# Tables built on Vector, head pairs transposed whole and Pool's mask product dropped in the first block of an attention + GLU kernel

## The chip, the cores and the metric

One core of one Trainium2 chip. The metric is the device time of one execution in microseconds; the number before is the median of four runs. One further execution was recorded by the hardware profiler; where the text gives a moment ("at 18.05"), it is counted in microseconds from the start of that execution's span.

## The reference

Two layers, one after the other. The first is a linear attention with decay, 4 batches, 8 heads, 768 positions, head dimension 64, one decay `lam` per head:

```python
for b in range(nb):                                   # blocks of positions
    intra = einsum('bhic,bhjc->bhij', qb, kb) * Dmask     # lam ** (i - j), lower triangle
    intra = einsum('bhij,bhjd->bhid', intra, vb)
    inter = einsum('bhid,bhde->bhie', qb * lam_pow, kv_state)   # lam ** (i + 1)
    out[:, :, sl] = intra + inter
    kv_state = lam_block * kv_state + einsum('bhsd,bhse->bhde', kb * rev_pow, vb)
```

The second takes the attention's output as 3072 tokens of width 512:

```python
gate = 1 / (1 + exp(-(x @ w_gate)))       # 512 x 1536
return (gate * (x @ w_val)) @ w_out       # 1536 x 512, float32
```

## The kernel before

Positions go in six units of 128 (`n` = 0 to 5, the text also says Block 0, unit 1 and so on), all four batches in each. The order of the instructions on every engine is the order in which the program writes them down; nothing reorders them.

**Attention of one unit.** q and k are transposed, so that the head dimension lies on the partitions: heads in two halves of 64 partitions (`u`), and per half four heads. `QS` is q transposed and scaled by `lamq` (lam to the power position + 1), `KS` k transposed. `piece_s` multiplies them into `sp0` and `sp1` (one per `u`, 128 x 512 each), `piece_m` multiplies by `mask` into `MT`, `piece_a` or `piece_a0` (Block 0, which has no state yet) multiplies with v and copies the result to `XT`. `make_kd` scales k for the state, `c` adds it to the state `Sb`, `fade` decays the state by `dec`.

**GLU of one unit.** For each of twelve column slices `ft` of 128: four matmuls with `WG` into `gp` (L399, L413 or L434), a sigmoid on Scalar, four with `WV` into `vp` (L405, L413, L440), the product `ht` on Vector. Then `piece_po` multiplies `ht` with `WO` and stores.

**Block 0** is written out by hand (L473 to L513), to get TensorE to the weights early. q's first two batches come as float32 by the Scalar and SP queues (`q0f`, `q1f`) and are cast by Vector; all else comes through Pool's queue, which converts to bfloat16 on the way, in this order: k batches 0-1, four Pool operations that build `jn`, `ident`, `ip1` and `tri` (L131 to L136), k 2-3, q 2, q 3, v 0, v 1, v 2, WG columns 0-127, v 3, WV columns 0-127. Further down in Pool's queue come the mask product of L282 (`piece_m2`: for batch 1, half `u` = 1, Scalar copies the scores to SBUF and Pool multiplies), then WG and WV columns 128-255 and the following slices, `make_kd(0)`, and unit 1's q, k and v.

`idle(n)` issues n matmuls of zeros, whose result nobody reads. `transpose` turns one head (128 x 64) at a time, two into the two halves of the result:

```python
def head(g, u):
    return 4 * (g % 2) + 2 * u + g // 2
```

With this order of heads `lamq`, `mask`, `MT` and the transposed tensors have one layout in all units. Units 1 (second half) and later are transposed by DMA on SP's queue (`transpose_half`, `transpose_by_dma`, L207: `QR` and `KR`), because their q and k are loaded with even and odd heads apart.

The tables: `jn` holds -1 - p and 127 - p by partition p; `ip1` is 1 to 128 along the free dimension; Scalar makes `lnp`, `lamq` (four exponentials), `lnl`, `pk`, `kds`, `dec` of them, and Vector multiplies `tri` by `pk` into `mask`.

Of the kernel before, what the change touches and what calls it, by code (L numbers as in the profile page):

```python
# [7 lines left out]

FP32 = mybir.dt.float32
BF16 = mybir.dt.bfloat16  # L10
AF = mybir.ActivationFunctionType
ALU = mybir.AluOpType
# [4 lines left out]
def kernel(  # L17
# [11 lines left out]
    nc = tc.nc  # L29

    B, H, S, D = q.shape
    C = 128
    NSTEP = S // C
    HP = H // 2
# [7 lines left out]
    const = ctx.enter_context(tc.tile_pool(name="const", bufs=1))  # L42
# [3 lines left out]
    mtp = ctx.enter_context(tc.tile_pool(name="mtp", bufs=4))  # L46
# [12 lines left out]
    lam_bc = const.tile([128, H], FP32, tag="lam_bc")  # L59
    nc.sync.dma_start(out=lam_bc, in_=lam.partition_broadcast(128))  # L60

    WG = const.tile([128, NMT, DFF], BF16, tag="WG")
    WV = const.tile([128, NMT, DFF], BF16, tag="WV")
    WO = const.tile([128, NFT, DM], BF16, tag="WO")
    wg_r = moe_w_gate.rearrange("(mt p) f -> p mt f", p=128)
    wv_r = moe_w_val.rearrange("(mt p) f -> p mt f", p=128)
    wo_r = moe_w_out.rearrange("(ft p) m -> p ft m", p=128)

    Q, K, V = {}, {}, {}
# [31 lines left out]
    def load_w(t, src, i, w):  # L101
        fs = slice(i * w, (i + 1) * w)
        nc.gpsimd.dma_start(out=t[:, :, fs], in_=src[:, :, fs])  # L103

    def load_gv(i, w):
        load_w(WG, wg_r, i, w)
        load_w(WV, wv_r, i, w)
# [5 lines left out]
    q01 = [const.tile([128, H, D], FP32, tag=f"q{b}f", name=f"q{b}f") for b in range(2)]  # L113
# [4 lines left out]
    ident = const.tile([128, 128], BF16, tag="ident")  # L118
    zero = const.tile([128, TCH], BF16, tag="zero")
    jn = const.tile([128, 2], FP32, tag="jn")  # L120
    ip1 = const.tile([128, C], FP32, tag="ip1")
    tri = const.tile([128, C], FP32, tag="tri")
    nc.vector.memset(zero, 0.0)
    nc.vector.memset(ident, 0.0)
    nc.vector.memset(tri, 0.0)
    Sb = stp.tile([128, B, HP, D], BF16, tag="Sb", name="Sb")
    nc.vector.memset(Sb, 0.0)

    load(0, "k", 0, 2)
    for i, base in enumerate((-1, C - 1)):  # L130
        nc.gpsimd.iota(jn[:, i:i + 1], pattern=[[0, 1]], base=base, channel_multiplier=-1,  # L131
                       allow_small_or_imprecise_dtypes=True)
    make_identity(nc, ident, nomemset=True)
    nc.gpsimd.iota(ip1, pattern=[[1, C]], base=1, channel_multiplier=0,
                   allow_small_or_imprecise_dtypes=True)
    nc.gpsimd.affine_select(out=tri, in_=tri, compare_op=ALU.is_gt, fill=1.0, base=0,  # L136
                            pattern=[[-1, C]], channel_multiplier=1)
    load(0, "k", 2, 4)
    load(0, "q", 2, 3)
    load(0, "q", 3, 4)  # L140
# [3 lines left out]
    GW = DFF // 6  # L144
    load_w(WG, wg_r, 0, GW // 2)
    load(0, "v", 3, 4)
    load_w(WV, wv_r, 0, GW // 2)

    lnp = const.tile([128, HP], FP32, tag="lnp")
    for u in range(2):  # L150
        us = slice(u * 64, (u + 1) * 64)
        nc.scalar.activation(lnp[us, :].rearrange("p (e x) -> p e x", e=2),
                             lam_bc[us, :].rearrange("p (x u e) -> p u e x", u=2, e=2)[:, u], AF.Ln)
    lamq = const.tile([128, HP, C], BF16, tag="lamq")
    for hp in range(HP):
        nc.scalar.activation(lamq[:, hp, :], ip1, AF.Exp, scale=lnp[:, hp:hp + 1])
    lnl = const.tile([128, H], FP32, tag="lnl")
    nc.scalar.activation(lnl, lam_bc, AF.Ln)
    pk = const.tile([128, H], FP32, tag="pk")
    nc.scalar.activation(pk, lnl, AF.Exp, scale=jn[:, 0:1])  # L160
    kds = const.tile([128, H], FP32, tag="kds")
    nc.scalar.activation(kds, lnl, AF.Exp, scale=jn[:, 1:2])
    dec = const.tile([128, HP], FP32, tag="dec")
    nc.scalar.activation(dec, lnp, AF.Exp, scale=float(C))
    nc.scalar.preload_act_table_set("sigmoid_and_others")
    mask = const.tile([128, 2, HP, C], FP32, tag="mask")

    def make_mask(u):
        nc.vector.tensor_tensor(
            out=mask[:, u].rearrange("p (e x) c -> p e x c", e=2),  # L170
            in0=tri.unsqueeze(1).unsqueeze(1).to_broadcast([128, 2, 2, C]),
            in1=pk.rearrange("p (x u e) -> p u e x", u=2, e=2)[:, u].unsqueeze(3).to_broadcast([128, 2, 2, C]),
            op=ALU.mult)

    def half(e):
        return slice(e * 64, (e + 1) * 64)
# [4 lines left out]
    def transpose(out, x, b, g):  # L181
        for u in range(2):
            nc.tensor.transpose(out[half(u)], x[:, b, head(g, u), :], ident)
# [3 lines left out]
    def idle(n):  # L187
        for i in range(n):
            nc.tensor.matmul(wm, lhsT=zero[:, :128], rhs=zero, start=True, stop=True,
                             skip_group_check=True)  # L190

    QS, KS, MT, XT, KD = {}, {}, {}, {}, {}
# [17 lines left out]
            KS[n, bp] = kt[:, :, 2 * bp:2 * bp + 2]  # L210

    lamq_e = lamq.rearrange("p (e x) c -> p e (x c)", e=2)

    def scale(n, bp, src):
        QS[n, bp] = trsb.tile([128, 2, 2, 2, C], BF16, tag="QS", name="QS")
# [4 lines left out]
    def piece_tq0(bs, then=None):  # L220
        tq = ps_at.tile([128, 2, 2, 2 * C], BF16, name="tq", tag="ps")
        for b in bs:
            if (0, b // 2) not in QS:
                QS[0, b // 2] = trsb.tile([128, 2, 2, 2, C], BF16, tag="QS", name="QS")
            for g in range(HP):
                transpose(tq[:, b % 2, g // 2, g % 2 * C:g % 2 * C + C], Q[0], b, g)
        if then:
            then()
        for b in bs:
            nc.vector.tensor_tensor(out=QS[0, b // 2][:, :, b % 2].rearrange("p e x c -> p e (x c)"),  # L230
                                    in0=tq[:, b % 2], in1=lamq_e, op=ALU.mult)

    def piece_tk0(bp):
        tk = ps_at.tile([128, 2, 2, 2 * C], BF16, name="tk", tag="ps")
        for i in range(2):
            for g in range(HP):
                transpose(tk[:, i, g // 2, g % 2 * C:g % 2 * C + C], K[0], 2 * bp + i, g)
        KS[0, bp] = trsb.tile([128, 2, 2, 2, C], BF16, tag="KS", name="KS")
        for i in range(2):
            cp = nc.vector.tensor_copy if bp == 0 and i == 0 else nc.scalar.copy  # L240
            cp(KS[0, bp][:, :, i].rearrange("p e x c -> p e (x c)"), tk[:, i])
# [18 lines left out]
    SP = {}  # L260
# [11 lines left out]
                                     start=(hp == 0), stop=(hp == HP - 1), skip_group_check=True)  # L272
            SP[n, b] = sp

    def piece_m2(n, b, part):
        if part:
            nc.vector.tensor_tensor(out=MT[n, b][:, 0], in0=SP[n, b][0], in1=mask[:, 0], op=ALU.mult)
            return
        MT[n, b] = mtp.tile([128, 2, HP, C], BF16, tag="MT", name="MT")
        sc = const.tile([128, HP, C], FP32, tag="sc", bufs=2)  # L280
        nc.scalar.copy(sc, SP[n, b][1])
        nc.gpsimd.tensor_tensor(out=MT[n, b][:, 1], in0=sc, in1=mask[:, 1], op=ALU.mult)  # L282

    def piece_m(n, b):
        MT[n, b] = mtp.tile([128, 2, HP, C], BF16, tag="MT", name="MT")
        for u in range(2):
            nc.vector.tensor_tensor(out=MT[n, b][:, u], in0=SP[n, b][u], in1=mask[:, u], op=ALU.mult)  # L287

    def intra(n, b, out, m, start, stop):
        for e in range(2):  # L290
            nc.tensor.matmul(out[half(e)], lhsT=V[n][:, b, 2 * m + e, :],  # L291
                             rhs=MT[n, b][:, m % 2, 2 * e + m // 2, :],
                             start=start, stop=stop, skip_group_check=True)

    def piece_a(n, pairs):
# [23 lines left out]
    def piece_a0(b, split=False):  # L319
        if 0 not in XT:  # L320
            XT[0] = xtp.tile([128, NMT, B, C], BF16, tag="XT", name="XT")
        w = 2 if split else NMT
        for m0 in range(0, NMT, w):
            op = ps_at.tile([128, w, C], FP32, name="op", tag="ps")
            for m in range(w):
                intra(0, b, op[:, m, :], m0 + m, m == 0, m == w - 1)
            if split and m0:
                nc.vector.tensor_copy(XT[0][:, m0:m0 + w, b, :], op)
            else:
                nc.scalar.copy(XT[0][:, m0:m0 + w, b, :], op)  # L330
# [139 lines left out]
            nc.sync.dma_start(out=out[lo:lo + rows, :], in_=ob[i * rows:(i + 1) * rows, :])  # L470


    idle(10)  # L473
    nc.vector.tensor_copy(Q[0][:, 0], q01[0])
    piece_tq0([0])
    nc.vector.tensor_copy(Q[0][:, 1], q01[1])
    idle(1)
    piece_tq0([1], lambda: make_mask(0))
    make_mask(1)
    idle(1)  # L480
    piece_tk0(0)
    idle(1)
    piece_s(0, [0])
    piece_m(0, 0)
    piece_s(0, [1])
    piece_m2(0, 1, 0)
    piece_m2(0, 1, 1)
    load_w(WG, wg_r, 1, GW // 2)
    load_w(WV, wv_r, 1, GW // 2)
    load_gv(1, GW)  # L490
    load_gv(2, GW)
    piece_tk0(1)
    piece_tq0([2])
    idle(1)
    piece_tq0([3])
# [3 lines left out]
    piece_m(0, 3)  # L499
    piece_a0(0)  # L500
    piece_a0(1)
    idle(1)
    piece_a0(2, True)
    idle(1)
    g0 = psum()
    mm_part(g0, WG, 0, 0, 0, 3 * C)
    piece_a0(3, True)
# [28 lines left out]
    def gv(n, *fts):  # L536
        for ft in fts:
            piece_gv(n, ft)
# [3 lines left out]
            piece_gvh(n, ft, i)  # L542

    gv(0, 1)
    gs = {}
    for ft in (2, 3):
        gs[ft] = psum()
# [115 lines left out]
```

## Time and profile before

| | |
|---|---|
| median of 4 runs | 228.12 us (227.67 to 228.4) |
| the profiled execution | 227.94 us, span 226.2 us |
| granted TensorE clock | 1.0 |
| TensorE busy | 217.5 us, 96% of the span |
| Vector, Scalar, Pool busy | 98.5, 79.3, 82.9 us |
| matmuls L399, L405, L462 (128x512) | 57.9, 57.6, 61.3 us, 379 ns each as recorded |
| mask products L287 on Vector | 46 of 682 ns |
| mask product L282 on Pool | 1 of 1352 ns, at 11.39 |
| TensorE's first matmul of L399 | at 18.05 us |
| last step of the chain of waits | L456 on Vector, at 223.28 us |

A line of a timeline reads: start in us, length in us, engine, line of the program, operation, result and operands, shape, count; in brackets the idle time of the engine just before it and what ended that. "PE" is TensorE's matmuls, "PEld" its weight loads, "DVE" Vector, "ACT" Scalar, "POOL" GpSimd, "SPq" the SP queue. Matmuls overlap in their recorded lengths, so their pace is read from starts, not from lengths. A group of matmuls may show fewer than it has, where records are missing.

### The profile page before, as it was taken

The page shows a single profiled execution, that of the slowest core. Times are in us where ns is not written, and L with a number is a line of the kernel's source. Part 1 is how long each engine was busy: PE and PEld are TensorE (multiplying, and loading weights), DVE is VectorE, ACT ScalarE, POOL GpSimd, SP SyncE. Part 2 cuts the span into 40 slices and gives each one's busy share as a digit, 9 for nine tenths or more (in the row PEclk, how much of TensorE's full clock was granted, in tenths as well). Part 3 has the DMA queues.
Part 4 walks back from the last instruction along what each step waited for, and adds up shares of the span by engine and source line. Part 5 has one row for each costly group of instructions (what it writes and reads, how often), then busy time and mean ns, then how long its engine had stood idle before and what let it go on. Part 6 is the DMA issues. An engine that isn't in the chain of part 4 may idle for free.

```text
span 226.2 us, 4318 instructions
## 1 busy us (share of the span) xinstructions
PE 217.5 (96%) x1772; PEld 114.8 (51%) x1796; DVE 98.5 (44%) x167; ACT 79.3 (35%) x149; POOL 82.9 (37%) x82
## 2 busy tenths in 40 slices
PE   7779999999999999999999999999999999999994
PEld 2444445788864445444446444446444445444443
DVE  2772647476422532445642335842334850343300
ACT  5544243435432225333115433225333224433221
POOL 7999987993394006940005950000000000000000
DMA  6999999999999994999221899921930012100022
GB/s 110 151 163 193 168 189 157 141 191 176 156 114 173 221 209 113 192 158 149 10 93 49 184 147 148 35 82 61 165 68 0 3 46 96 46 0 0 0 96 94
DMA packets 105861, 25.72 MB, mean 114 GB/s; under 512 B 95985, under 2 KB 102897, under 8 KB 105841
## 3 DMA queue, kind: packets, MB, share of 16 engines
q0 software_dynamic: 81232, 13.90, 95.8%
q1 hardware_dynamic: 23568, 11.28, 22.8%
q10 hardware_dynamic: 1040, 0.26, 0.5%
q8 instruction: 14, 0.23, 0.5%
q14 instruction: 7, 0.05, 0.1%
HBM read 28.32 MB, written 6.29 MB: 153 GB/s over the span
## 4 chain that ended last, share of the span: by engine, by line
PE 66%; DMA 17%; POOL 11%; SPq 2%; DVE 2%; issue 1%; DVEq 0%
PE po L462 22%; PE gp L399 19%; PE vp L405 18%; DMA qb<-in_q_dram 6%; DMA KR<-kb 5%; DMA kb<-in_k_dram 4%; SPq L207 2%; POOL WV L103 2%; PE sp L270 2%; POOL WG L103 2%; DMA q0f<-in_q_dram 2%; PE op L291 2%; POOL kd L337 2%; PE po L451 1%; PE op L303 1%; POOL WO L111 1%
## 5 line engine op out<-in xcount | busy, mean ns | idle before, releaser
L408 DVE TENSOR_TENSOR ht<-sg,vp 128x512 bf16<-128x512 bf16 x57 | 39.2, 687 | 68.7 <-PE vp L405 64.6
L462 PE MATMUL po<-WO,ht 128*128 128x512 bf16 x266 | 61.3, 379 | 0.5
L399 PE MATMUL gp<-XT,WG 128*128 128x512 bf16 x221 | 57.9, 379 | 1.0 <-DMA WG<-in_moe_w_gate_dram 0.4
L405 PE MATMUL vp<-XT,WV 128*128 128x512 bf16 x223 | 57.6, 379 | 0.1
L402 ACT ACTIVATE sg<-gp 128x512 bf16<-128x512 f32 x57 | 34.0, 597 | 62.9 <-PE gp L399 61.7
L462 PEld LDWEIGHTS <-ht 128*128 128x128 bf16 x276 | 26.3, 98 | 31.0
L405 PEld LDWEIGHTS <-WV 128*128 128x128 bf16 x228 | 22.3, 98 | 26.9
L399 PEld LDWEIGHTS <-WG 128*128 128x128 bf16 x228 | 21.7, 98 | 26.2 <-DMA WG<-in_moe_w_gate_dram 0.6
L287 DVE TENSOR_TENSOR MT<-sp,mask 128x512 bf16<-128x512 f32 x46 | 29.0, 682 | 8.7 <-PE sp L270 8.7
L465 ACT COPY ob<-po 128x512 f32<-128x512 f32 x23 | 13.5, 586 | 52.5 <-PE po L462 48.6
L364 POOL TENSOR_TENSOR sd<-Sb,dec 128x512 f32<-128x512 bf16 x8 | 8.1, 1037 | 40.8 <-DVE Sb L390 40.8
L434 PE MATMUL gp<-XT,WG 128*128 128x256 bf16 x96 | 14.4, 273 | 0.0
L440 PE MATMUL vp<-XT,WV 128*128 128x256 bf16 x96 | 14.4, 273 | 0.0
L444 DVE TENSOR_TENSOR ht<-sg,vp 128x256 bf16<-128x256 bf16 x24 | 10.0, 420 | 8.6 <-PE vp L440 8.6
L437 ACT ACTIVATE sg<-gp 128x256 bf16<-128x256 f32 x24 | 9.2, 384 | 12.6 <-PE gp L434 11.5
L97 POOL DMA_DIRECT2D vb<-in_v_dram x10 | 12.8, 1290 | 1.7 <-issue 1.1
L355 POOL TENSOR_TENSOR kd<-kb,kds 128x1024 bf16<-128x1024 bf16 x6 | 11.3, 1907 | 4.7 <-PE vp L440 4.7
L390 DVE TENSOR_TENSOR Sb<-cp,sd 128x512 bf16<-128x512 f32 x8 | 5.2, 686 | 15.5 <-PE cp L383 15.5
L317 ACT CAST XT<-op 128x512 bf16<-128x512 f32 x20 | 10.4, 597 | 3.0 <-PE op L291 3.0
L434 PEld LDWEIGHTS <-WG 128*128 128x128 bf16 x96 | 9.2, 98 | 1.7 <-issue 0.2
L440 PEld LDWEIGHTS <-WV 128*128 128x128 bf16 x96 | 9.4, 98 | 1.1
L78 POOL DMA_DIRECT2D qb<-in_q_dram x8 | 9.4, 1182 | 0.0
(77 smaller groups left out, 142.0 us busy)
## 6 DMA issues: line engine op xcount, KB each, us to landing
out_dram<-ob SPq DMA_DIRECT2D x21, 256.0 KB, 2.0
kb<-in_k_dram POOLq DMA_DIRECT2D x11, 256.0 KB, 9.7
qb<-in_q_dram POOLq DMA_DIRECT2D x9, 256.0 KB, 8.6
vb<-in_v_dram POOLq DMA_DIRECT2D x4, 512.0 KB, 14.8
WO<-in_moe_w_out_dram POOLq DMA_DIRECT2D x3, 512.0 KB, 9.1
WG<-in_moe_w_gate_dram POOLq DMA_DIRECT2D x5, 256.0 KB, 7.0
WV<-in_moe_w_val_dram POOLq DMA_DIRECT2D x5, 256.0 KB, 7.6
qb<-in_q_dram POOLq DMA_DIRECT2D x4, 128.0 KB, 7.8
```

Source lines behind the costliest of these rows:

```text
L97: nc.gpsimd.dma_start(out=lst[n][:, b0:b1], in_=src[b0:b1, :, sl, :].rearrange("b h s d -> s (b h) d"))
L287: nc.vector.tensor_tensor(out=MT[n, b][:, u], in0=SP[n, b][u], in1=mask[:, u], op=ALU.mult)
L317: nc.scalar.copy(XT[n][:, u::2, 2 * bp:2 * bp + 2, :], OP[bp, u])
L355: nc.gpsimd.tensor_tensor(out=KD[n][:, e], in0=K[n][:, e], in1=kds[:, e::2].unsqueeze(1).unsqueeze(3).to_broadcast([128, B, HP, D]), op=AL ...
L399: nc.tensor.matmul(gp, lhsT=WG[:, mt, fs], rhs=x[:, mt, :], start=(mt == 0), stop=(mt == NMT - 1))
L402: nc.scalar.activation(sg, gp, AF.Sigmoid)
L405: nc.tensor.matmul(vp, lhsT=WV[:, mt, fs], rhs=x[:, mt, :], start=(mt == 0), stop=(mt == NMT - 1))
L408: nc.vector.tensor_mul(HT[n, ft], sg, vp)
L434: nc.tensor.matmul(gp[:, cs], lhsT=WG[:, mt, fs], rhs=x[:, mt, cs], start=(mt == 0), stop=(mt == NMT - 1))
L440: nc.tensor.matmul(vp[:, cs], lhsT=WV[:, mt, fs], rhs=x[:, mt, cs], start=(mt == 0), stop=(mt == NMT - 1))
L462: nc.tensor.matmul(po, lhsT=HT[n, ft][:, tt * 128:(tt + 1) * 128], rhs=WO[:, ft, :], start=(ft == 0), stop=(ft == NFT - 1))
L465: nc.scalar.copy(ob, po)
```

## The change

1. `jn`, `ident`, `ip1` and `tri` are built on Vector instead of Pool: `ip1` by seven doubling additions from a column of ones, the partition index `p1` from a 32x32 block transpose of it and four additions, the rest by comparison with `p1`. The memsets of `ident`, `tri` and `Sb` go.
2. WG and WV columns 128-255 and the two slices after them are issued directly behind the loads, and Pool's mask product (`piece_m2`) is gone: batch 1 uses `piece_m` as the others do.
3. Block 0 keeps the natural order of heads: neighbouring heads 2g and 2g + 1 are transposed in one 128x128 transpose (`transpose_pair`). It has its own `lamq0`; the later units' `lamq` is made on Vector by doubling products (`make_lamq`), after `gv(0, 1)`. `mask` lies in natural order too, and later units read it through a strided view (`masked`).
4. Scalar casts q's second batch, its sigmoid table is loaded after the first K copies, `make_mask(0)` moves ahead of the first QS product, `piece_a0(2)` is no longer split in two, and the idle matmuls are set anew.

```diff
-    nc.vector.memset(ident, 0.0)
-    nc.vector.memset(tri, 0.0)
     Sb = stp.tile([128, B, HP, D], BF16, tag="Sb", name="Sb")
-    nc.vector.memset(Sb, 0.0)
+    nc.vector.memset(ip1[:, 0:1], 1.0)
+    w = 1
+    while w < C:
+        nc.vector.tensor_scalar_add(ip1[:, w:2 * w], ip1[:, 0:w], float(w))
+        w *= 2
+    loc = const.tile([128, 32], FP32, tag="loc")
+    nc.vector.transpose(loc, ip1[:, 0:32])
+    p1 = const.tile([128, 1], FP32, tag="p1")
+    for lo in range(0, 128, 32):
+        nc.vector.tensor_scalar_add(p1[lo:lo + 32], loc[lo:lo + 32, 0:1], float(lo))
+    nc.vector.tensor_scalar(out=ident, in0=ip1, scalar1=p1, scalar2=None, op0=ALU.is_equal)
+    for i, base in enumerate((0.0, float(C))):
+        nc.vector.tensor_scalar(out=jn[:, i:i + 1], in0=p1, scalar1=-1.0, scalar2=base,
+                                op0=ALU.mult, op1=ALU.add)
+    nc.vector.tensor_scalar(out=tri, in0=ip1, scalar1=p1, scalar2=None, op0=ALU.is_ge)
 
     load(0, "k", 0, 2)
-    for i, base in enumerate((-1, C - 1)):
-        nc.gpsimd.iota(jn[:, i:i + 1], pattern=[[0, 1]], base=base, channel_multiplier=-1,
...
-    make_identity(nc, ident, nomemset=True)
-    nc.gpsimd.iota(ip1, pattern=[[1, C]], base=1, channel_multiplier=0,
...
-    nc.gpsimd.affine_select(out=tri, in_=tri, compare_op=ALU.is_gt, fill=1.0, base=0,
...
     load_w(WV, wv_r, 0, GW // 2)
+    load_w(WG, wg_r, 1, GW // 2)
+    load_w(WV, wv_r, 1, GW // 2)
+
     lnl = const.tile([128, H], FP32, tag="lnl")
     nc.scalar.activation(lnl, lam_bc, AF.Ln)
     pk = const.tile([128, H], FP32, tag="pk")
     nc.scalar.activation(pk, lnl, AF.Exp, scale=jn[:, 0:1])
...
+        nc.scalar.activation(lnp[us, :], lam_bc[us, u::2], AF.Ln)
+    lamq0 = const.tile([128, HP, C], BF16, tag="lamq0")
+    for hp in range(HP):
+        nc.scalar.activation(lamq0[:, hp, :], ip1, AF.Exp, scale=lnp[:, hp:hp + 1])
+    nc.scalar.copy(Q[0][:, 1], q01[1])
...
-    nc.scalar.activation(dec, lnp, AF.Exp, scale=float(C))
-    nc.scalar.preload_act_table_set("sigmoid_and_others")
-    mask = const.tile([128, 2, HP, C], FP32, tag="mask")
+    for u in range(2):
+        us = slice(u * 64, (u + 1) * 64)
+        nc.scalar.activation(dec[us, :].rearrange("p (e x) -> p e x", e=2),
...
+    mask = const.tile([128, H, C], FP32, tag="mask")
+
+    def make_lamq():
+        lp = const.tile([128, HP, C], FP32, tag="lp")
+        for u in range(2):
+            us = slice(u * 64, (u + 1) * 64)
+            nc.vector.tensor_copy(lp[us].rearrange("p (e x) c -> p e x c", e=2)[:, :, :, 0],
...
+        w = 1
+        while w < C:
+            nc.vector.tensor_tensor(out=lp[:, :, w:2 * w], in0=lp[:, :, 0:w],
+                                    in1=lp[:, :, w - 1:w].to_broadcast([128, HP, w]), op=ALU.mult)
+            w *= 2
+        nc.vector.tensor_copy(lamq, lp)
...
+    def masked(out, x, n, u):
+        if n == 0:
+            nc.vector.tensor_tensor(out=out, in0=x, in1=mask[:, u::2, :], op=ALU.mult)
+            return
+        nc.vector.tensor_tensor(
+            out=out.rearrange("p (e x) c -> p e x c", e=2), in0=x.rearrange("p (e x) c -> p e x c", e=2),
+            in1=mask.rearrange("p (x u e) c -> p u e x c", u=2, e=2)[:, u], op=ALU.mult)
...
+    def transpose_pair(out, x, b, g):
+        nc.tensor.transpose(out, x[:, b, 2 * g:2 * g + 2, :].rearrange("p h d -> p (h d)"), ident)
...
-    def piece_m2(n, b, part):
...
+    load_gv(1, GW)
+    load_gv(2, GW)
+
     idle(10)
     nc.vector.tensor_copy(Q[0][:, 0], q01[0])
-    piece_tq0([0])
-    nc.vector.tensor_copy(Q[0][:, 1], q01[1])
-    idle(1)
-    piece_tq0([1], lambda: make_mask(0))
+    piece_tq0([0], lambda: make_mask(0))
     make_mask(1)
     idle(1)
+    piece_tq0([1])
     piece_tk0(0)
     idle(1)
     piece_s(0, [0])
     piece_m(0, 0)
     piece_s(0, [1])
-    piece_m2(0, 1, 0)
-    piece_m2(0, 1, 1)
-    load_w(WG, wg_r, 1, GW // 2)
-    load_w(WV, wv_r, 1, GW // 2)
-    load_gv(1, GW)
-    load_gv(2, GW)
+    piece_m(0, 1)
     piece_tk0(1)
+    nc.scalar.preload_act_table_set("sigmoid_and_others")
+    idle(1)
     piece_tq0([2])
...
-    idle(1)
-    piece_a0(2, True)
-    idle(1)
+    idle(2)
+    piece_a0(2)
+    idle(2)
     g0 = psum()
...
     gv(0, 1)
+    make_lamq()
     gs = {}
```

## The prediction

> **What bounds the kernel now.** First the page: TensorE is busy in 96% of the span, and its busy strip is full from the third slice on.
>
> ```profile
> PE 217.5 (96%) x1772; PEld 114.8 (51%) x1796; DVE 98.5 (44%) x167; ACT 79.3 (35%) x149; POOL 82.9 (37%) x82
> ...
> PE   7779999999999999999999999999999999999994
> ...
> DMA  6999999999999994999221899921930012100022
> ...
> q0 software_dynamic: 81232, 13.90, 95.8%
> ...
> q8 instruction: 14, 0.23, 0.5%
> ```
>
> So a change in Block 0 (the first 18 us) can only move the start of one long TensorE run. Where does that run wait? The timeline of TensorE, then of its weight loads:
>
> ```profile
> 17.28 0.39 PE L413 MATMUL gp<-XT,WV 128*128 128x128 bf16 x4
> 18.05 1.04 PE L399 MATMUL gp<-XT,WG 128*128 128x512 bf16 x4 [0.38 <-DMA WG<-in_moe_w_gate_dram]
> 18.92 1.03 PE L405 MATMUL vp<-XT,WV 128*128 128x512 bf16 x4
> ...
> 19.96 0.55 PEld L413 LDWEIGHTS <-WG 128*128 128x128 bf16 x4 [0.51 <-DMA WG<-in_moe_w_gate_dram]
> ...
> 74.91 0.45 PEld L270 LDWEIGHTS <-KR 64*128 64x128 bf16 x16 [0.63 <-DMA KR<-kb]
> ```
>
> All three are transfers. By issue times the gaps are: 17.50 (last of v0, 17.445 plus a pitch of 0.056) to 18.05, 0.54 us; 19.78 to 19.97, 0.19; and 74.62 (48 matmuls of 0.216 from 64.25) to 74.91, 0.29. Together 1.02 us; after that the chain of waits shows TensorE alone. The chain also says that the third gap hangs on transfers, not on TensorE:
>
> ```profile
> 30.45 9.54 DMA kb<-in_k_dram
> 39.99 0.07 issue
> 40.06 2.06 POOL kd L349 x2
> ...
> 63.66 11.21 DMA KR<-kb
> 74.87 0.05 issue
> 74.91 0.62 PE sp L270 x16
> ```
>
> Then the DMA side. The packet records show the software queue carrying about 600 packets of 128 B, or 190 of 512 B, per 0.5 us without a hole from 4.5 to 41 us. It is saturated: issuing earlier does not make it deliver earlier. The sixteen completions of each transfer add one thing. Up to the first WV slice the last of the sixteen comes 0.2 us after the median (16.35 against 16.21). From the next slice, WG's columns 128 to 255, it is 1.36 late (18.00 against 16.64), and stays over 1 late until 41 us. What happened between:
>
> ```profile
> q0 software_dynamic: 207, 0.05, 173.3%
> q8 instruction: 1, 0.02, 25.9%
> ```
>
> That is the DMA view at 15.3 to 15.6 us: one 16 KB instruction packet at 15.45, lasting 1.24 us, on an engine that carries the weights. The two early gaps are that packet.
>
> **The change, part by part.** The sum is made against the profiled execution, 227.94 us (span 226.2 and 1.74 around it), 0.18 under the median of 228.12.
>
> *Tables.* Pool loses two iotas for jn, the ident select, the ip1 iota and the tri select (2.63 to 3.49, 0.86 us); Vector loses the memsets of ident, tri and Sb (0.11 + 0.17 + 0.48) and gains 17 small operations: a memset, seven doublings, the transpose, four offsets, ident, two jn, tri. Nearest rows: the 128x64 memset at 0.11 and the 128x128 one at 0.165. At 0.11 to 0.2 each they end between 3.0 and 4.5; Vector then waits for q0f until 5.00. Nothing; at 0.25 each it would be 0.4 us late. No gain either.
>
> A rule speaks against this part. Pool's first K issue lasts 1.28 us beside Vector's memsets and the second, alone, 1.19: 0.09 for the overlap. The Trainium skill ("SBUF — State Buffer", "SBUF: two separate sides") says that a Vector operation in a two-port mode locks GpSimd out of their shared port, so that it can't write descriptors; the next section there ("A bandwidth-pool intuition that's wrong (but worth ruling out)") has a DMA of about 620 ns take about 3100 beside one. By the row the first K transfer is 0 to 0.3 us late, by the rule up to 2.5 (my estimate, the difference of its two figures), and the whole stream with it. I take the row, 0: the K packets start at 4.45, just as q0f's packets end. The rule is a rival below.
>
> *Pool's queue.* The 1.35 us mask product goes, and WG's and WV's second slices follow WV's first directly. Eight semaphores serve these transfers in turn (at 31.77 Pool waits with eight in flight), so WG's second slice is issued when q's third batch lands, at 10.75 instead of 12.61; the slices after it, make_kd(0) and load(1) come about 1.4 us earlier. With a saturated stream in the same order: 0 for the landings, 0.4 us at best (the stream ran some 5% under its best rate from 8.5 to 14.5). SP's queue keeps its order.
>
> *Block 0 on Vector and Scalar.* Scalar casts q1f (0.6 us; lands 6.25) right after lamq0, at about 6.25 to 6.85, where Vector did it at 6.96 to 7.56. Vector goes cast, mask, QS, mask, QS and is free at 7.8, but K lands at 8.05, so the first KS copy moves only from 9.01 to about 8.65 to 8.95. Then Vector's rows:
>
> ```profile
> 9.92 1.29 DVE L287 TENSOR_TENSOR MT<-sp,mask 128x512 bf16<-128x512 f32 x2 [0.49 <-PE sp L270]
> 11.12 0.68 DVE L277 TENSOR_TENSOR MT<-sp,mask 128x512 bf16<-128x512 f32 x1
> 11.72 0.86 DVE L230 TENSOR_TENSOR QS<-tq,lamq 128x512 bf16<-128x512 bf16 x2
> 12.60 2.48 DVE L287 TENSOR_TENSOR MT<-sp,mask 128x512 bf16<-128x512 f32 x4
> ```
>
> Pool's half of batch 1 is now Vector's, one more product at a pitch of 0.60. From a KS copy at 8.65 to 8.95: first product 9.56 to 9.86, four to 11.96 to 12.26, QS twice, next product 12.83 to 13.13, last one done 15.3 to 15.6 (before 15.08). It is wanted by a0(3), which waits for v's fourth batch, 15.79, anyway. a0(2) is no longer split: one cast of 0.59 in place of 0.37 and 0.41 side by side, so g0 starts at 15.43 instead of 15.09 and a0(3) at 16.1 instead of 15.88. v0 waits for WV's first slice, 16.35, in both. TensorE is through Block 0 at 17.5, as before: 0. If this cover goes (Vector over 0.3 us later still), it comes straight onto TensorE.
>
> *TensorE.* The 64 half transposes become 32 whole ones. Halves start in pairs 0.056 apart and whole 128-column matmuls 0.056 apart (g0's last part): 0. Two idle matmuls more, 2 x 0.216, fill waits for v and for the cast.
>
> *Elsewhere.* Scalar's sigmoid table (1.28) moves from 6.39 to about 11.8, ending before the first XT cast at 13.4; dec costs a second 0.2, off the path. make_lamq puts two copies, seven products of 4 to 256 elements and a cast on Vector at 20.7: by the 512-element product (0.60 pitch) 1.5 and 0.6, some 2.3 us, between products at 20.05 and 22.84; the next ht is at worst 0.4 late, and vp of ft 4, which needs its bank, comes only at 24.29. The mask's strided view in the later products: make_mask's four-level pattern took 0.677 where flat products take 0.682, so 0 (bounds 0 and 0.1 each, under TensorE either way).
>
> *Instruction packets.* TensorE's 3568 instructions come in 14 packets, 255 apiece. The row says that one costs a weight engine 1.24 us; the Trainium skill ("Runtime: NRT & Kernel Launch", "Instruction fetch mechanics") says 256 per 16 KiB block, and that crossing a block is mostly hidden. By the rule moving a packet is worth 0; by the row it moves a wall. I go by the row. TensorE has 64 transpose instructions fewer and 4 idle ones more, so every packet comes 60 instructions later: the first at about 19.2 instead of 15.45. WG's second slice then lands at about 16.9 and the next at 18.9: gaps one and two vanish. But the packet makes the engine late again before WV's columns 512 to 767, which land at 23.96 as before and are used at 24.29. So TensorE runs from 17.5 and is stopped there: 24.29 - 23.96 = 0.33 gained, not 0.73.
> The packet at 65.26 (2.25 us) lies in the QR transpose, whose packets all but stop from 66.0 to 67.5. 60 instructions later is about 71 us, with QR and KR through some 2.5 us sooner: the third gap, 0.29, goes too.
>
> Sum: 227.94 - 0.33 - 0.29 = 227.32; with 0.18 to the median, 227.5 us.
>
> **The rivals.** A measurement of this kernel can tell about 0.3% (0.68 us) from no change, so 227.5 lies just inside.
> *A, the forecast* (0.52): 226.9 to 227.9; faster in 0.20, same in 0.32.
> *B, repaid at KR* (0.08): KR's landing stays at 74.87, pinned by K of unit 1 at 40 us; what is gained before becomes a longer wait there. 228.1. For it: the chain. Against: the packet that stalled QR moves.
> *C, a bigger step* (0.21): the moved packet is short (the one at 29.27 took 0.95) or the stream delivers earlier through Pool's lead; all three gaps go: 228.12 - 1.02 = 227.1.
> *D, slower* (0.19): the port rule holds. The seventeen Vector operations starve the first K issue at 1.26 us; K, and every transfer behind it, is late by x, Block 0 and KR with it. Slower than before from x = 0.62, measurably from 1.3; at x = 1.5, 228.12 - 0.62 + 1.5 = 229.0. Against it: 0.09 us in the one overlap that shows.
> Faster 0.20 + 0.21, same 0.32 + 0.08, slower 0.19. Range 226.9 to 228.9: C's lower bounds and most of D.
>
> **What would show it.** Right: the first 16 KB packet near 19 us, L399's first matmul at about 17.5 with no DMA wait, a new short one before L405 near 24, none at KR, QR landing before 68. Wrong: a first K issue well over 1.3 us or K landing after 8.3 (D); a wait at KR over 0.5 us (B); TensorE leaving Block 0 after 17.8 with Vector as the releaser.

## The result and the profile after

The changed kernel takes 227.15 us (median of 37 runs, 227.05 to 228.77; 35 of them between 227.05 and 227.48). The kernel before, run beside it, takes 228.27 us (median of 56, 227.64 to 230.75). The ratio is 0.9944, with a 95% interval of 0.9932 to 0.9955. By it the change is worth 1.3 us, by the medians 1.1, by the fastest runs 0.6. These differ because the kernel before scatters more: the middle half of its runs lies between 228.02 and 228.86, that of the changed kernel between 227.09 and 227.23. In the runs made beside the later experiments the kernel before once took 227.24, so a lucky execution of it comes within 0.2 us of the changed one.

The profiled execution of the changed kernel was an uncommon one of 228.06 us, so the profile of a second run of the same kernel, 227.15 us, stands beside it and is called "the repeat" below. Its page:

```profile
span 225.4 us, 4273 instructions
PE 217.1 (96%) x1742; PEld 114.6 (51%) x1766; DVE 103.9 (46%) x190; ACT 79.7 (35%) x150; POOL 80.8 (36%) x76
...
PE   7789999999999999999999999999999999999994
...
q0 software_dynamic: 81232, 13.90, 80.7%
...
q8 instruction: 14, 0.23, 0.4%
```

TensorE is as full as before, and its work is the same. One number moved that nothing in the change speaks of: the same 81232 packets of the software queue take 80.7% of sixteen engines' span, where they took 95.8%. The experiments come back to it.

The timeline of TensorE in the repeat, from the end of Block 0, then at KR:

```profile
16.83 0.39 PE L436 MATMUL gp<-XT,WV 128*128 128x128 bf16 x4
17.06 1.03 PE L422 MATMUL gp<-XT,WG 128*128 128x512 bf16 x4
17.92 1.03 PE L428 MATMUL vp<-XT,WV 128*128 128x512 bf16 x4
19.20 1.04 PE L436 MATMUL gp<-XT,WG 128*128 128x512 bf16 x4 [0.25 <-DMA WG<-in_moe_w_gate_dram]
...
22.66 1.03 PE L422 MATMUL gp<-XT,WG 128*128 128x512 bf16 x3
23.77 1.02 PE L428 MATMUL vp<-XT,WV 128*128 128x512 bf16 x4
...
70.62 3.62 PE L485 MATMUL po<-WO,ht 128*128 128x512 bf16 x16
74.17 0.62 PE L302 MATMUL sp<-QS,KR 64*128 64x128 bf16 x16
```

L422 is the old L399, L428 the old L405, L436 the old L413. Each time in front is to be set against the row of the same matmul before: 17.06 against 18.05, 19.20 against 19.97, 23.77 against 24.29, 74.17 against 74.91. So 0.77 us are won by 19.2, a quarter of a microsecond is lost again at 23.77, and the stop at KR is gone. The span is 0.8 shorter. In the changed kernel's other, slower profile the same stretch reads:

```profile
17.05 1.03 PE L422 MATMUL gp<-XT,WG 128*128 128x512 bf16 x4
18.80 1.04 PE L428 MATMUL vp<-XT,WV 128*128 128x512 bf16 x4 [0.71 <-DMA WV<-in_moe_w_val_dram]
19.67 1.89 PE L436 MATMUL gp<-XT,WG 128*128 128x512 bf16 x8
...
24.61 0.59 PE L428 MATMUL vp<-XT,WV 128*128 128x512 bf16 x2 [0.46 <-DVE ht L449]
```

It leaves Block 0 at the same time, and then stands for WV's columns 128 to 255: they landed at 18.75 here and at 17.14 in the repeat. Both profiles have a 16 KB instruction packet at 16.7 us, so its time of arrival alone does not decide what comes late.

The packet records show one more difference. For the q, k and v pieces of Block 0 it took 0.9 to 1.1 us before from a transfer's last completion packet (the small packet that reports the end) to its landing, the last of the sixteen completions (the first K piece: packet at 7.08, landing at 8.05), and 0.33 to 0.4 in the repeat (7.08 and 7.43). The packets themselves came at the same time at first, and up to 0.35 us earlier later on (WV's first slice, 15.60 and 15.25). The K piece is 0.6 us earlier for the completions alone, v's fourth batch 0.9 (15.79, 14.93) and WV's first slice 0.7 (16.35, 15.65).

### The profile page after: what moved, and what is told of

Its sections match the earlier page's. It is cut to its first block, busy times and chain, and to the rows that moved or that the text cites. A ratio compares the mean times of both kernels' runs of the same rounds, so it can differ in the third digit from the quotient of the medians.

```text
span 226.2 us, 4273 instructions
## 1 busy us (share of the span) xinstructions
PE 217.1 (96%) x1742; PEld 114.5 (51%) x1766; DVE 103.8 (46%) x190; ACT 79.7 (35%) x150; POOL 80.9 (36%) x76
## 3 DMA queue, kind: packets, MB, share of 16 engines
q0 software_dynamic: 81232, 13.90, 79.7%
## 4 chain that ended last, share of the span: by engine, by line
PE 88%; POOL 4%; DMA 3%; DVE 2%; issue 1%; DVEq 0%; POOLq 0%
PE po L485 26%; PE vp L428 22%; PE gp L422 21%; PE gp L457 5%; PE vp L463 5%; DMA WV<-in_moe_w_val_dram 3%; PE sp L302 2%; PE op L314 2%; POOL vb L96 2%; PE op L326 1%; PE cp L406 1%; PE po L474 1%; POOL kb L96 1%; POOL qb L96 1%; DVE lp L185 1%
## 5 line engine op out<-in xcount | busy, mean ns | idle before, releaser
L428 PE MATMUL vp<-XT,WV 128*128 128x512 bf16 x223 | 57.6, 379 | 1.3 <-DMA WV<-in_moe_w_val_dram 0.7
L422 PE MATMUL gp<-XT,WG 128*128 128x512 bf16 x221 | 57.9, 379 | 0.6 <-issue 0.2
L428 PEld LDWEIGHTS <-WV 128*128 128x128 bf16 x228 | 22.2, 98 | 28.5 <-DMA WV<-in_moe_w_val_dram 1.2
L422 PEld LDWEIGHTS <-WG 128*128 128x128 bf16 x228 | 21.7, 98 | 25.7
L199 DVE TENSOR_TENSOR MT<-sp,mask 128x512 bf16<-128x512 f32 x40 | 25.2, 682 | 10.8 <-PE sp L302 10.8
L460 ACT ACTIVATE sg<-gp 128x256 bf16<-128x256 f32 x24 | 9.2, 384 | 12.6 <-PE gp L457 11.5
L413 DVE TENSOR_TENSOR Sb<-cp,sd 128x512 bf16<-128x512 f32 x8 | 5.2, 686 | 15.5 <-PE cp L406 15.5
```

The lines of the kernel that those rows point to most:

```text
L199: nc.vector.tensor_tensor(out=out.rearrange("p (e x) c -> p e x c", e=2), in0=x.rearrange("p (e x) c -> p e x c", e=2), in1=mask.rearrange ...
L422: nc.tensor.matmul(gp, lhsT=WG[:, mt, fs], rhs=x[:, mt, :], start=(mt == 0), stop=(mt == NMT - 1))
L428: nc.tensor.matmul(vp, lhsT=WV[:, mt, fs], rhs=x[:, mt, :], start=(mt == 0), stop=(mt == NMT - 1))
```

## The experiments

Five theories, with the letters that the expectations use. R: where a 16 KB instruction packet falls decides which weight slice comes late, and for how long. C: the late completions of the kernel before are chance, or belong to the chip. A: they belong to the place of the tiles. The program's allocation has qb, kb and vb at bytes 69216, 85600 and 101984 of each partition before, 32 past a multiple of 64, and at 68352, 84736 and 101120 after, multiples of 64, because the new small tables take other room. P: Pool's second K issue, which runs at 3.49 to 4.68 before and ends by 3.70 after, since no tables stand ahead of it. L: make_lamq holds Vector, and with it ht and TensorE.

**The two kernels again.** The kernel before, unchanged:

> The kernel before, once more, for a second profile. Ratio to the kernel before 1.000. Theory R (instruction packets on a weight-carrying DMA engine make TensorE wait): the first 16 KB packet lies again between 14 and 17 us, and the transfer in flight then lands over 1 us after the median of its sixteen completions. Theory C (the profile of before happened to have late completions): the 1.07 us between the last completion packet of the first K transfer and its landing falls to about 0.33, as in the profile after. If C, part of the step in landings between the two profiles is chance of one execution; if the 1.07 is there again, it belongs to the kernel.

Measured: 228.51 us (227.76 to 230.17), ratio 1.0001 [0.9968, 1.0034]. Completions again 0.9 to 1.05 after the packet, a 16 KB packet at 15.68, WG's columns 128 to 255 at 18.15. So both belong to the kernel; C falls. The changed kernel, unchanged:

> The kernel after, once more, for a second profile. Its profiled execution took 228.06 us, but most of its executions take 227.05 to 227.25. Theory R: in an execution of the common kind the first 16 KB packet lies elsewhere than 16.7 us, WV's second slice lands by 18.0 instead of 18.75, and TensorE has no DMA wait before L428; the wait for ht before the fifth vp (0.46 as recorded) stays. Rival: the wait on WV's second slice is there in all executions, and the 0.9 us lie elsewhere. Ratio to the kernel before 0.993 to 0.996.

Measured: 227.19 us (227.07 to 227.36), ratio 0.9945 [0.9917, 0.9973]; its profile is the repeat shown above. R expected the 16 KB packet elsewhere than at 16.7 and WV's columns 128 to 255 landed by 18.0 with no stop. The packet is at 16.70 again, and the landing is at 17.14 with no stop: half of that forecast came.

**The instruction stream.** The changed kernel with the whole transposes of Block 0 split into halves again, so that TensorE's instructions are 64 more:

```
-        nc.tensor.transpose(out, x[:, b, 2 * g:2 * g + 2, :].rearrange("p h d -> p (h d)"), ident)
+        for u in range(2):
+            nc.tensor.transpose(out[half(u)], x[:, b, 2 * g + u, :], ident)
```

> The kernel after, with the 32 whole transposes of Block 0 split into 64 half ones again: same data, same layout, same time on TensorE (pairs start 0.056 us apart), but 64 more TensorE instructions ahead of every later instruction packet. Theory R: the packets go back by 64 instructions and the time moves by 0.3 to 1.0 us, most likely up, to a ratio of about 0.998 to 1.000 to the kernel before. Rival P (the gain is Pool's lead and the earlier stream): no change against the kernel after, ratio 0.994.

Measured: two groups and nothing between them, seven runs at 227.08 to 227.30 and five at 228.56 to 228.62 (median 227.24; ratio over all 0.997 [0.994, 1.0], which holds both forecasts). The profile is of the second group; its first 16 KB packet is at 15.08, 1.6 us earlier than with whole transposes. Its timeline of TensorE:

```profile
15.62 0.41 PE L315 MATMUL op<-MT,vb 128*64 128x128 bf16 x8
17.15 0.82 PE L437 MATMUL gp<-XT,WV 128*128 128x384 bf16 x4 [1.12 <-DMA WV<-in_moe_w_val_dram]
```

WV's first slice, wanted at 16.0, landed at 17.11, though the median of its sixteen completions is at 15.38: one engine was 1.7 late. TensorE stood 1.12 us. That fits R: a packet at about 15 can come with a stop of over a microsecond, or with none (14.96 in the kernel before with tables on Vector, below). The link is one of time. In each of the thirteen profiles the last completion falls further behind the median, by 0.4 to 1.7 us, at a transfer that is in flight when the first 16 KB packet comes; but the records do not name the DMA engine of a packet. The whole transposes do not shorten TensorE's own way there (it is through with L315 at 16.03 here, and with the same matmuls at 16.02 in the repeat); they move the packet to 16.7. That the first group's runs are those in which the packet falls on another engine was not shown, as none of them was profiled.

**make_lamq.** In three parts, behind ft 1, 4 and 5 (one loop is cut into its factors, nothing else):

```
-    make_lamq()
+    make_lamq(0)
     ... ft 4
+    make_lamq(1)
     ... ft 5
+    make_lamq(2)
```

> The kernel after, with make_lamq issued in three parts (after ft 1, ft 4 and ft 5) instead of in one piece after ft 1. Theory L: the 3.3 us of small Vector operations hold back the products of ft 2 and 3, whose bank the fifth vp needs; TensorE waits 0.6 us there in every execution, and that is the floor of 227.1. Then this kernel takes 226.5 us, ratio 0.991 to 0.992. Rival W (the weights' landings hold TensorE anyway): WV's columns 512 to 767 land at about 23.5, so at most 0.2 us is gained, ratio 0.993 to 0.994.

Measured: 227.25 us (227.15 to 227.7), ratio 0.9943 [0.9915, 0.997]; the 226.5 that L expected did not come. The timeline of TensorE:

```profile
23.48 1.03 PE L429 MATMUL vp<-XT,WV 128*128 128x512 bf16 x4
...
27.12 0.81 PE L423 MATMUL gp<-XT,WG 128*128 128x512 bf16 x3 [0.16 <-DVE Sb L412]
```

The stop at 23.77 is gone, and comes back 3 us later: Vector's copy of Sb now stands behind the third part. So the parts went behind ft 1, 5 and 6:

> The kernel after with make_lamq in three parts again, the second after ft 5 and the third after ft 6, so that none stands before the copies of the state (with the parts after ft 4 and 5 TensorE won 0.29 at the fifth vp and waited for Sb's copy in place of it). Theory L: 0.25 to 0.3 us less than the kernel after, 226.9 us, ratio 0.993. Rival W: KR, which then comes next, or WG's slices hold TensorE at the same place; 227.2 us.

Measured: 226.86 to 227.46 us (median 227.2 of 9), ratio 0.9929 [0.9901, 0.9957]; the profiled execution took 226.95, and KR starts at 73.89 instead of 74.17. L is right in the profile, where the stop is gone and 0.28 us is won by KR. The medians (227.19, 227.2) do not show it: these nine runs lie 0.6 us apart.

**Address and tables, in both bodies.** A tile of 32 bytes that nothing uses, ahead of mask, shifts mask and every tile behind it by 32 bytes, qb, kb and vb among them. On the kernel before that aligns them:

```
+    pad = const.tile([128, 8], FP32, tag="pad")
     mask = const.tile(...)
```

> The kernel before, with one unused tile of 32 bytes per partition ahead of mask: every later tile (qb, kb, vb, QS, MT, QR, KR and so on) moves from an address 32 bytes off a multiple of 64 to a multiple of 64, where the kernel after has them by chance of its new tiles. No instruction changes. Theory A (alignment): 128-byte writes that start 32 bytes off drain slowly; the 1.0 us between last completion packet and landing falls to 0.33 us, v's fourth batch lands at about 15.0 instead of 15.74, WG's second slice about 0.7 earlier, and the time falls by 0.3 to 0.8 us, ratio 0.9965 to 0.9985. Rival P (Pool's lead, or the tables, makes the stream land earlier): nothing moves, ratio 1.000.

On the changed kernel the same line takes the alignment away:

> The kernel after with the same 32 bytes ahead of mask, which takes its tiles off the multiples of 64 again. Theory A: landings late by 0.7 us again between 7 and 15 us, and TensorE, which leaves Block 0 at 17.05, leaves it at 17.5 to 17.7; ratio 0.9965 to 0.998 to the kernel before. Rival P: no change against the kernel after, ratio 0.9945.

The changed kernel with the tables back on Pool between its two K issues, written as before, and padded so that the tiles stay aligned:

> The kernel after with the four tables built on Pool again, behind the first K issue, and with ident, tri and Sb set to zero on Vector; 32 bytes of padding keep qb, kb and vb on multiples of 64. Theory A with R: Pool's second K issue is 0.86 us later, the landings stay within 0.1 us (the stream is saturated), Vector is free of its port waits; the time stays, ratio 0.994 to 0.995. Rival P: landings 0.5 to 0.9 later from the second K transfer on, ratio 0.997 to 0.999.

And the kernel before with nothing but the tables put on Vector, where the tiles come to lie aligned without a pad, and the same with the pad, which misaligns them:

> The kernel before with only the tables moved to Vector; with the new small tiles the q, k and v tiles come to start at multiples of 64 bytes, as in the changed kernel. Heads aren't paired, the weights' second slices stay where they were, and lamq stays on Scalar. Theory T (an early second K issue and early completions are all of the gain): about 227.2 us, TensorE leaves Block 0 near 17.1 without a stop. Theory R (they only pay where the 16 KB instruction packet, which comes as TensorE's instruction stream reaches a place, falls late enough; without the paired transposes the stream is about 30 matmuls longer and the packet stays near 15): the packet lands on a first weight slice, a stop of 0.5 to 1.1 us near 17, and 227.8 to 228.3 us, with the wide spread of the kernel before.

> As the run before, and a 32-byte tile that nothing uses moves the q, k and v tiles 32 bytes off a multiple of 64. Theory A (the start of the tile sets how long a transfer's completion takes): completions at 0.9 to 1.1 us after the last packet instead of 0.33, first K piece at about 8.0 instead of 7.4. The time by T: 0.7 to 0.9 more than the aligned one; by R: within 0.4 of it, as the stop on the weights is there in both.

Measured, with the profiled executions' own marks (us): when TensorE leaves Block 0, when WG's columns 256 to 511 land, when their first matmul runs, and when KR's does.

| body | tables | tiles | median (fastest) | profiled | leaves | WG lands | used | KR |
|---|---|---|---|---|---|---|---|---|
| before | Pool | 32 off | 228.27 (227.64) | 227.94 | 18.05 | 19.92 | 19.97 | 74.91 |
| before | Pool | aligned | 228.24 (227.67) | 227.74 | 18.23 | 19.52 | 19.96 | 74.75 |
| before | Vector | 32 off | 228.28 (227.42) | 228.39 | 18.18 | 20.11 | 20.16 | 75.36 |
| before | Vector | aligned | 227.36 (227.09) | 227.20 | 17.29 | 19.15 | 19.20 | 74.19 |
| changed | Vector | 32 off | 228.04 (227.96) | 228.31 | 18.74 | 20.07 | 20.46 | 75.20 |
| changed | Pool | aligned | 227.84 (227.75) | 227.76 | 17.38 | 19.50 | 19.55 | 74.77 |
| changed | Vector | aligned | 227.19 (227.07) | 227.15 | 17.06 | 19.15 | 19.20 | 74.17 |

Ratios to the kernel before, from the second row down: 0.9991 [0.9966, 1.0015], 0.9994 [0.9967, 1.002], 0.996 [0.9936, 0.9984], 0.9973 [0.9952, 0.9995], 0.9974 [0.9956, 0.9992], and 0.9945 [0.9917, 0.9973] for the last. The profiles of the third and the fifth row ran for some microseconds at half of TensorE's clock (last section).

Three of the forecasts failed. For the second row A had the completions right and the time wrong (0.9965 to 0.9985 expected). For the fifth, TensorE was to leave Block 0 at 17.5 to 17.7. For the sixth, A with R had 0.994 to 0.995 and landings within 0.1 us; the measured 0.9974 is what P expected.

What follows, first for A. Each of the four aligned profiles has 0.28 to 0.35 us from packet to completion at the first K piece and 7.34 to 7.43 as its landing; each of the three others has 0.85 to 0.97, and 7.97 to 8.05. The windows view shows it without any packet record. Its last two columns are the DMA engines' busy share (in packets at a time per engine) and GB/s, here at 9.5 to 11.5 us; first the kernel before, then the same with the 32-byte tile:

```profile
9.50:11.50 2.00, 1.57 (x40) 1.23 (x41) 1.58 (x3) 1.48 (x3) 2.00 (x4) 1.00 3.22 146
```

```profile
9.50:11.50 2.00, 1.57 (x40) 1.23 (x41) 1.59 (x3) 1.48 (x3) 2.00 (x4) 1.00 2.43 155
```

The reader is to see that nothing differs but the two last numbers: a packet holds its engine a third longer, and 6% fewer bytes come through. The kernel before with tables on Vector has the same pair, without and with the pad:

```profile
9.50:11.50 2.00, 1.53 (x42) 1.19 (x43) 1.63 (x3) 1.48 (x3) 1.34 (x3) 1.00 2.42 154
```

```profile
9.50:11.50 2.00, 1.99 (x27) 1.21 (x28) 1.30 (x3) 0.96 (x2) 1.04 (x2) 0.50 3.20 147
```

A is shown for the completions: one unused tile turns their delay on and off in both bodies, and the page's q0 share goes with it (79.5 to 81.8% in the four aligned rows of the table, 90.3 to 98.2% in the three others). What it is worth in time is another question.

Then P. With aligned tiles and the tables on Pool, the second K piece lands at 9.44 and 9.68 in the two bodies; with the tables on Vector at 9.08 and 9.09. The median completion is at 8.8 to 8.9 in all four: it is one engine of the sixteen that is later by 0.35 to 0.6 us. It stays late in every transfer after it, up to WG's columns 256 to 511, which land at 19.5 instead of 19.15. That last step is not P's alone. Two profiles with tables on Vector and aligned tiles, the slower one of the changed kernel and the one with halves, have no such engine at the second K piece (9.05 and 9.04), and land that slice at 19.49 and 19.46 all the same, behind their 16 KB packets. Why one engine falls behind when the second issue is late, and why it doesn't show with the tiles 32 off, no run settles. These runs move all of the tables, so they test P with everything else that the tables' place changes; that the lateness begins with the second K piece is what speaks for P.

Then the time. By medians neither alignment alone (228.24) nor early tables alone (228.28) helps the kernel before, and both together take 0.9 us off it; in the changed body each of the two is missed by 0.65 to 0.85. What they share is the column "WG lands": in this table it is 19.15 only with both. The medians do not speak for every execution: three of the ten runs of the third row took 227.42 to 227.51. In five of the seven rows the first matmul on that slice follows its landing by 0.05 us: it is a wall, and its move from 19.92 to 19.15 is the 0.77 of the column "used". In the two other rows something else is later still. In one, the changed kernel with the tiles 32 off, it is TensorE itself, of which more below; in the other, the kernel before with the pad, a packet at 14.99 hits a first slice, and TensorE stands ahead of

```profile
17.13 0.82 PE L414 MATMUL gp<-XT,WV 128*128 128x384 bf16 x4 [0.83 <-DMA WV<-in_moe_w_val_dram]
```

Theory T of the later expectations (A and P are all of the gain) is right in the main: 227.36 against 227.19 in the medians. R, which had 227.8 to 228.3 for the kernel before with tables on Vector, is right on its packet (14.96), which made WG's columns 128 to 255 late (17.22) by too little to stop anything, and on the spread: 3 of 12 runs of the kernel before with tables on Vector are at 228.3 to 228.5, and only 2 of all 47 of the changed kernel are over 228. Paired transposes, the lead of Pool's second slices and Scalar's lamq0 together buy some 0.2 us at most in the medians; the steadiness fits the later packet, but was not taken apart further. Nor is the kernel before with tables on Vector free of small stops: without make_lamq it is at the fifth vp at 23.53, 0.24 ahead of the repeat, and loses 0.25 ahead of a vp at 32.52, where the trace shows no releaser. So both are at KR at 74.2, and the 0.2 us are not in the profiles.

**A version beyond both.** The three parts of make_lamq behind ft 1, 5 and 6, and Scalar making lnp and lamq0 ahead of lnl and pk:

```
-    lnl, pk ...          (ahead of lnp)
     lnp, lamq0 ...
+    lnl, pk ...
```

> The changed kernel with lamq made in three parts behind ft 1, 5 and 6, and Scalar making lnp and lamq0 before lnl and pk, so that lamq0 doesn't wait behind pk for jn. If the wait of QS for lamq0 (0.50 us) is on the path to Block 1: 226.6 to 226.8. If K's landing ends the same stage anyway: as with the three parts alone, 226.9 to 227.2.

Measured: 226.94 us (226.82 to 227.48, 12 runs), ratio 0.9938 [0.9915, 0.9962], the lowest median here. Against the three parts alone the fastest run is 0.04 lower and the median 0.26, but the two were not run side by side. The new order has little to win, and the timeline of TensorE says why:

```profile
16.89 1.03 PE L423 MATMUL gp<-XT,WG 128*128 128x512 bf16 x4
17.76 1.03 PE L429 MATMUL vp<-XT,WV 128*128 128x512 bf16 x4
19.23 1.04 PE L437 MATMUL gp<-XT,WG 128*128 128x512 bf16 x4 [0.44 <-DMA WG<-in_moe_w_gate_dram]
```

It leaves Block 0 0.17 earlier than the changed kernel and stands 0.19 longer at the same wall.

## Why the prediction was right or wrong

The sign and the range were right, the size was short, and the mechanism only half right. Against its own base, the profiled 227.94, it forecast 0.62 us less, and the repeat's profile has 0.79 less; the medians are 1.1 apart. The measured 227.15 is rival C's number, but not its way: of its three gaps only two went, and neither of its two causes is the one found (the lead of Pool's slices is missing in the kernel before with tables on Vector, which meets the same landing at 19.15).

That the range held is in part luck. At the weights the forecast's 0.33 was to come from the moved instruction packet. The kernel before with tables on Vector, whose packet stays at 14.96, has the same landing at 19.15; and completions and tables, to which the seven rows tie that landing, stood in the sum at 0. Of the signs that the prediction named, three came: no stop before the first matmul of L399 (now L422), none at KR, QR before 68. Two did not: a packet near 19, and a stop on a transfer near 24. Step by step:

*"0 for the landings" was the term that was mis-sized.* The stream is saturated and its packets come within 0.35 us of when they came before; so far the reading held. But TensorE waits for completions, and these are 0.6 to 0.9 us earlier. The step took the two for one. The change in their distance, at the first K piece 0.97 to 0.35, comes from where the new tables push the tiles, which the diff doesn't say. The 1 us from packet to landing was there to be read in the trace of before, and so was the 0.3 (by the medians) of WG's and WV's slices from WG's columns 256 to 511 on, which lie 32 off in both kernels, but with 512-byte packets. The steps "Pool's queue" and "Block 0 on Vector and Scalar", 0 each, stand in their sum. Not in every reading: Scalar's cast of q1f starts at 6.69 and not at 6.25, and TensorE waits 0.71 for it at 7.34 in the repeat; but being through Block 0 earlier has no worth.

*Tables, "nothing, no gain", was wrong.* With aligned tiles they are worth 0.65 us in the changed body (227.84 to 227.19) and 0.9 in the old (228.24 to 227.36); by what way, is open (P above). It was argued from a saturated stream again. Their price on Vector was under the truth too: they end at 5.0, not at 3.0 to 4.5. Of the seven doublings five took 0.154 to 0.182 us and two 0.73. The groups on Vector, in the repeat's timeline:

```profile
1.19 2.52 DVE L127 TENSOR_SCALAR ip<-ip 128x1 f32<-128x1 f32 x7
3.08 0.63 DVE L130 STREAM_TRANSPOSE loc<-ip 128x32 f32<-128x32 f32 x1
...
4.61 0.21 DVE L136 TENSOR_SCALAR jn<-p 128x1 f32<-128x1 f32 x2
4.74 0.28 DVE L138 TENSOR_SCALAR tri<-ip,p 128x128 f32<-128x128 f32 x1
5.00 0.72 DVE L500 CAST qb<-q0f 128x512 bf16<-128x512 f32 x1
```

Vector is just done when q0f lands, so its path hides that; Scalar waits 0.79 for jn, and QS 0.50 for lamq0 in turn.

*The port rule (rival D) was weighed rightly, in the half that it was weighed for.* The repeat's row of Pool:

```profile
1.26 2.44 POOL L96 DMA_DIRECT2D kb<-in_k_dram  x2 [0.81 <-POOLq L669]
```

Two issues in 2.44 us, 1.22 each, beside the Vector rows above: Pool is not held up. The rule of the Trainium skill ("SBUF — State Buffer", "SBUF: two separate sides") has a lock that whoever comes first keeps. It fits what happened to Vector. The two long doublings end at 2.52 and 3.72, Pool's issues at 2.55 and 3.70. A copy in make_lamq, further down, takes 0.93 and ends at 20.58, as Pool's product kd ends at 20.55; in the changed kernel with the tiles 32 off, where kd ends at 21.36 and the copies start at 21.34, the two copies take 0.16 and 0.17. So Vector is the one that stands, by 0.55 to 0.75 us. The ends and that one run agree with the rule; no run took Pool's issues away from beside the doublings.

*Instruction packets: the direction was right, the size not.* They come later with fewer instructions, but the first at 16.7 instead of 19.2. The 64 instructions are worth 1.6 us of the stream there (15.08 to 16.70 by the run with halves), where the prediction had 60 for 3.75. So gap one vanishes (0.54, WG's columns 128 to 255), and gap two does not. Counted by issue times, as the prediction counts, it grows from 0.19 to 0.42 us (18.78 to 19.20; the bracket of the timeline has 0.25), as WG's columns 256 to 511 come late (19.15, with the median completion at 18.27). With the 0.44 us that TensorE leaves Block 0 earlier, 0.54 less 0.23 make up the 0.77 at 19.2. As to "mostly hidden" in the Trainium skill ("Runtime: NRT & Kernel Launch", "Instruction fetch mechanics"), stops of 0.83 and 1.12 us follow a packet in profiles shown here; as said, the link is one of time.

*The wall at WV's columns 512 to 767, 23.96, did not bind.* They land at 23.15. What stopped TensorE there was make_lamq, which the prediction had at 2.3 us and "nothing". It takes 3.4, in the repeat's timeline of Vector:

```profile
19.66 1.11 DVE L181 COPY lp<-lam_bc 64x4 f32<-64x4 f32 x2
20.80 1.85 DVE L185 TENSOR_TENSOR lp<-lp 128x4 f32<-128x4 f32 x7
22.69 0.43 DVE L188 CAST lamq<-lp 128x512 bf16<-128x512 f32 x1
23.03 1.27 DVE L449 TENSOR_TENSOR ht<-sg,gp 128x512 bf16<-128x512 bf16 x2
```

The two copies of 64x4 take 1.1 instead of about 0.4 (one of them 0.93, beside Pool's kd), and the first ht of the two comes at 23.03 for a vp that could start at 23.52. This costs 0.25. The forecast of that instant, 24.29 - 0.33 = 23.96, is near the measured 23.77 for other reasons than it gave.

*The third gap, 0.29, is gone as forecast.* QR lands at 66.99 and KR at 71.53 in the first profile after (69.49 and 74.87 before), and TensorE does not wait there. Rival B falls with that. The reason given, the packet at 65.26 for 2.25 us that was to move away, is not what the runs show: with halves it is at 65.86 for 1.18 and in the kernel before with the pad at 65.3 for 1.35, and KR does not wait in either. In the repeat, where it is at 68.2, QR is issued at 56.20 instead of 58.25 and KR lands at 71.12, 3.75 earlier; so over half of the lead was there before the packet. Of the rest, packet and addresses were not separated.

*TensorE's 17.5 at the end of Block 0* became 17.06, by the earlier landings of v and WV's first slice, and that 0.44 is nearly worthless: 17.29 in the kernel before with tables on Vector ends at the same 19.20.

## What to carry to other kernels

When the first matmuls of a kernel stand on transfers, read the distance from the last packet to the landing, and not only whether the queue is full: here it was 1.0 or 0.3 us with the same packets, and a 32-byte tile turned the one into the other. A new constant tile moves every tile that is allocated behind it, so a change of tables can be a change of addresses; run such a change with a pad that restores the old addresses before crediting its own idea. And look for the wall: bringing TensorE earlier to a slice that lands at 19.15 was worth nothing, moving the landing was worth nearly all of the change in the profiles.

## What was not expected of the hardware

128-byte packets into tiles that start 32 bytes past a multiple of 64: between 9.5 and 11.5 us a mean busy share of 3.2 instead of 2.4, 146 to 148 instead of 154 or 155 GB/s, completions 0.85 to 1.1 us after the last packet instead of about 0.3. WG's and WV's 512-byte packets, 32 off in all of these kernels, showed 0.25 to 0.35 by the medians once the 128-byte stream ahead of them was through. The runs move the tiles by 32 bytes only; other offsets and packet sizes were not tried.

The clock of TensorE could be suspected. In both kernels with tables on Vector and the tiles 32 off, the profiled executions have a granted clock of 0.50 between 9.5 and 11.5 us (a row above shows one), and the changed one leaves Block 0 at 18.74, the latest of all. Yet of its other runs, four with a mean clock of 1.0 took 228.00 to 228.10 us and seven with 0.992 took 227.96 to 228.27, so the clock does not explain that kernel's time. The kernel before has its tiles 32 off too, and a clock of 1.0 in its profile.

Behind a 16 KB instruction packet the last of a transfer's completions stays late: in the repeat it is 0.3 us behind the median before the packet at 16.7 us, and 0.8 to 1.3 after it, until about 40 us. Executions of one program can fall into two sharp groups 1.4 us apart, as the run with halves showed; that the packet divides them is likely, not shown.
